# A planned three-stage kernel (attention, PReLU MLP, Mish MLP): a higher planned price on TensorE's mode changes, and a new table of priorities

## The chip, the cores and the metric

The kernel runs on one core of a Trainium2 chip. A core has four compute engines with instruction streams of their own: TensorE (PE; matmuls, its weight loads are listed as PEld), VectorE (DVE), ScalarE (ACT) and GpSimd (POOL). SyncE (SP) issues the DMAs here. Engines wait for each other through semaphores. SBUF is the memory on the core, PSUM the eight banks that the matmuls write. The metric is the device time of one execution in microseconds (us); lower is better. About 0.2% (some 2.1 us) is what repeated measurement can tell from no change.

## The reference

Three computations follow each other, all in float32 (the weights arrive as 64-bit floats):

```python
# attention: B=4, H=8, S=576, D=64
scores = (q @ k.T) / sqrt(D)
cum    = cumsum(log(clip(f, 1e-4, 1)), axis=-1)
scores = where(causal, -1e9, scores + cum[..., :, None] - cum[..., None, :])
attn   = exp(scores - max(scores)); attn /= sum(attn) + 1e-9
x = (attn @ v) -> 2304 tokens x 512
# MLP 1: 512 -> 2048 -> 512
h = x @ w_in;  g = max(h, 0) + alpha * min(h, 0);  x = g @ w_out
# MLP 2: 512 -> 2048 -> 512
h = x @ w_in;  g = h * tanh(log1p(exp(min(h, 20))));  out = g @ w_out
```

## The kernel before

**Attention** works on 16 pairs of heads. `stage_M` (L616) makes the scores once only for the row maximum, which VectorE takes from the bank (L623); its banks are 4 to 6, "one" in the planner. L635 transposes the maxima. `stage_S` (L660) makes the scores again, with bias and maximum folded in, in banks 0 to 3; ScalarE's Exp (L670) reads them, GpSimd selects (L678) and adds (L696). `stage_R` (L708) makes the row sums, ScalarE inverts them (L713, L716), VectorE scales (L718, L721). `stage_V` (L742) multiplies by v in banks 4 to 6, and VectorE writes the result to X (L748).

TensorE runs in three tilings, which the planner calls modes: r (whole array: L616, L635 and all of the MLPs), k (halves of 64 rows: L660) and c (halves of 64 columns: L708, L742).

**The MLPs** run over blocks of 384 tokens (6 blocks) and chunks of 128 of the 2048 hidden features (16 chunks). Every float32 product is made of three matmuls, high by high, high by low and low by high parts: a chunk's first product takes 12 matmuls (L786, L787, L788 for each of 4 slices of 128), its second 12 in layer 1 (L851 to L853) and 9 wider ones in layer 2 (L862 to L864). Splitting into parts is a cast on ScalarE (L321) and a subtraction (L331, `minus`) on GpSimd or VectorE. A PReLU is a Relu on ScalarE (L805) or a minimum on VectorE (L807), then L811 or L814 on VectorE, then that split: cast (L321) and subtraction (L331) make the two parts of g, which the second product reads.

The first four chunks of layer 1 are "group A". For blocks 0 to 2 they run as filler between the matmuls of attention, through bank 7 alone; for blocks 3 to 5 they run after attention's end (about 276 to 340 us). Then come the other 12 chunks of layer 1, six blocks of them (72 PReLUs; stage `H0`; to about 600 us); L905 folds a block's four output banks into what group A left. Then layer 2 (stage `H1`).

**Weights** arrive as 64-bit floats and are made into 32-bit ones half a tile at a time by ScalarE (L399) and VectorE (L401, L403, L405) in two buffers, wb. During layer 1 the weights of layer 2 are converted too and stored to DRAM (L434, `wd<-wb`); L399 of the next tile in the same buffer waits until that store has landed.

**What sets the order.** No engine chooses anything at run time. Every operation is first noted by `Plan.add` (L66) with its engine, a cost and a due time; the due time is shifted by `PRIO[stage][n]` for the n-th operation of a stage (L20), and where an operation can go to several engines, `ENG` (L21) picks one. `Plan.schedule` (L96) then builds one fixed sequence by list scheduling, and all engines' programs are written in it. Two numbers speak of TensorE's modes: `STAY` (L39) is added to the due time of an operation whose mode is not the present one, and `SWITCH` (L38) is added to the planned end of an operation that changes it.

```python
choice = [(p[0][0] + (self.STAY if m[0] != now[e] else 0.0), m) for m, p in open_[e].items()
...
end = free[e] = s + cost[n] + (self.SWITCH if m[0] != now[e] else 0.0)
```

Of the kernel before, what the change touches and what calls it, by code (L numbers as in the profile page):

```python
# [1041 lines left out]
```

## Time and profile before

| | us |
|---|---|
| median of 3 runs (range) | 1057.97 (1057.28 to 1059.17) |
| the profiled execution's own time | 1058.0 |
| its span in the profile | 1056.2 |
| TensorE busy | 1017.5 (96%) |
| VectorE busy | 745.1 (71%) |
| ScalarE busy | 542.1 (51%) |
| GpSimd busy | 414.2 (39%) |

The span runs from the first to the last record; 1.8 us of the execution lie outside it. "Busy" counts instructions under way, so short gaps between matmuls of different kinds show as idle time. Of the waits that the views list, only those of TensorE lengthen the span directly.

### The profile page before, as it was taken

Reading aid. Unit: us, or ns where it says so; the run is one execution under the profiler, and the core shown is the slowest. Engines: PE = TensorE matmul, PEld = TensorE weight load, DVE = VectorE, ACT = ScalarE, POOL = GpSimd, SP = SyncE. Lnnn points to the kernel's source line nnn. Section 1 sums busy time; section 2 is a strip of 40 time slices with the busy share of each in tenths; the row PEclk is TensorE's granted clock in tenths of the full one; section 3 lists DMA queues with packets and bytes.
Section 4 is the critical chain, followed back from the end, with each engine's and each line's share of the span. In section 5 each row is a group of like instructions: output and inputs, shape, how many; then the busy total and the mean of one; then the engine's idle time right before and its main releaser. Section 6 shows DMA issues by size and latency. Waiting matters only on the chain.

```text
span 1056.2 us, 16992 instructions
## 1 busy us (share of the span) xinstructions
PE 1017.5 (96%) x5996; PEld 914.7 (87%) x5996; DVE 745.1 (71%) x1673; ACT 542.1 (51%) x1133; POOL 414.2 (39%) x423
## 2 busy tenths in 40 slices
PE   7989999999978999999999999999999999999998
PEld 7756677777778999999999999998999989999897
DVE  6587655656588767888612247979888788887885
ACT  4777656664454544444332336555455454554543
POOL 4575543553455562413232324242233322423231
PEclk9999999999999999999999999999999999999999
DMA  5233221210133345565500034100000000000000
GB/s 163 89 110 98 79 70 36 71 48 12 44 117 100 125 137 183 183 207 182 163 1 1 20 92 129 41 1 31 1 6 25 1 30 1 1 31 1 31 1 31
DMA packets 55399, 71.06 MB, mean 67 GB/s; under 512 B 6673, under 2 KB 32273, under 8 KB 55313
## 3 DMA queue, kind: packets, MB, share of 16 engines
q1 hardware_dynamic: 55312, 69.97, 21.2%
q8 instruction: 47, 0.77, 0.3%
q14 instruction: 40, 0.32, 0.1%
HBM read 56.60 MB, written 13.33 MB: 66 GB/s over the span
## 4 chain that ended last, share of the span: by engine, by line
PE 85%; DVE 6%; DMA 3%; ACT 2%; issue 2%; POOL 1%; SPq 0%; ACTq 0%; DVEq 0%; POOLq 0%
PE b L786 12%; PE b L787 11%; PE b L788 11%; PE b L660 6%; PE b L863 6%; PE b L862 6%; PE b L864 6%; PE b L851 5%; PE b L853 5%; PE b L852 5%; PE b L742 4%; PE b L616 3%; PE b L519 2%; DVE wb L403 2%; PE b L708 2%
## 5 line engine op out<-in xcount | busy, mean ns | idle before, releaser
L786 PE MATMUL b<-xh,w 128*128 128x384 f32 x768 | 261.1, 340 | 9.0 <-ACT x L321 5.4
L788 PE MATMUL b<-xl,w 128*128 128x384 f32 x768 | 258.7, 337 | 0.0
L787 PE MATMUL b<-xh,w 128*128 128x384 f32 x768 | 258.6, 337 | 0.0
L843 POOL TENSOR_TENSOR x<-x 128x384 f32<-128x384 f32 x96 | 112.5, 1172 | 246.6 <-DVE x L841 165.7
L786 PEld LDWEIGHTS b<-xh,w 128*128 128x128 f32 x768 | 145.2, 189 | 17.6 <-ACT x L321 6.4
L787 PEld LDWEIGHTS b<-xh,w 128*128 128x128 f32 x768 | 145.2, 189 | 4.0
L788 PEld LDWEIGHTS b<-xl,w 128*128 128x128 f32 x768 | 145.0, 189 | 0.0
L331 POOL TENSOR_TENSOR g<-X,g 128x384 fp32r<-128x384 f32 x72 | 78.6, 1095 | 164.8 <-ACT g L321 128.4
L851 PE MATMUL b<-g,w 128*128 128x384 f32 x384 | 131.8, 343 | 9.4 <-DVE x L811 2.5
L853 PE MATMUL b<-g,w 128*128 128x384 f32 x384 | 129.8, 338 | 0.7 <-POOL g L331 0.6
L852 PE MATMUL b<-g,w 128*128 128x384 f32 x384 | 129.3, 337 | 0.0
L321 ACT CAST g<-x 128x384 fp32r<-128x384 f32 x120 | 61.4, 512 | 115.5 <-POOL x L843 105.0
L864 PE MATMUL b<-w,g 128*128 128x512 f32 x288 | 113.2, 393 | 0.0
L863 PE MATMUL b<-w,g 128*128 128x512 f32 x288 | 113.2, 393 | 0.0
L862 PE MATMUL b<-w,g 128*128 128x512 f32 x288 | 113.1, 393 | 0.0
L811 DVE SCALAR_TENSOR_TENSOR X<-X,alph,b 128x384 f32<-128x384 f32 x72 | 43.9, 611 | 84.3 <-ACT X L805 83.8
L623 DVE CUSTOM_DVE_ANT_0 junk<-b,tri 128x320 f32<-128x320 f32 (+3 forms) x160 | 69.4, 434 | 45.8 <-PE b L616 33.2
L331 DVE TENSOR_TENSOR g<-x,g 128x384 fp32r<-128x384 f32 x102 | 74.9, 736 | 17.6 <-ACT g L321 17.3
L399 ACT ACTIVATE wb<-raw 128x256 f32<-128x256 f32 x128 | 52.2, 432 | 66.8 <-DMA wd<-wb 38.2
L851 PEld LDWEIGHTS b<-g,w 128*128 128x128 f32 x384 | 72.6, 189 | 13.8 <-DVE x L814 3.4
L805 ACT ACTIVATE X<-b 128x384 f32<-128x384 f32 x72 | 35.2, 489 | 88.7 <-PE b L788 88.0
L401 DVE TENSOR_SCALAR wb<-wb 128x256 int32<-128x256 int32 x128 | 55.1, 450 | 33.9 <-ACT wb L399 33.0
(93 smaller groups left out, 1973.7 us busy)
## 6 DMA issues: line engine op xcount, KB each, us to landing
raw<-in_moe_w_in_dram SPq DMA_DIRECT2D x64, 256.0 KB
raw<-in_moe_w_out_dram SPq DMA_DIRECT2D x64, 256.0 KB
wd<-wb SPq DMA_DIRECT2D x32, 256.0 KB
raw<-wd SPq DMA_DIRECT2D x32, 256.0 KB
qt<-in_q_dram SPq DMA_DIRECT2D x16, 288.0 KB
kt<-in_k_dram SPq DMA_DIRECT2D x16, 288.0 KB
out_dram<-x SPq DMA_DIRECT2D x18, 256.0 KB
vt<-in_v_dram SPq DMA_DIRECT2D x16, 256.0 KB
```

The costliest lines, as they stand in the source:

```text
L331: plan.add(engs, 0.0, at, lambda e: (nc.gpsimd if e == "POOL" else nc.vector).tensor_tensor(out=out(), in0=in0(), in1=in1(), op=ALU.subtra ...
L623: nc.vector.tensor_tensor_reduce(out=junk[ql, :z - a], in0=ps()[ql, :z - a], in1=tri[ql, x0 + a:x0 + z], scale=-1.0, scalar=BIG if n == 0 ...
L786: nc.tensor.matmul(ps[:, :NB], w[:, 0, c], xh[c], start=(c == 0), stop=False)
L787: nc.tensor.matmul(ps[:, :NB], w[:, 1, c], xh[c], start=False, stop=False)
L788: nc.tensor.matmul(ps[:, :NB], w[:, 0, c], xl[c], start=False, stop=(c == KC - 1))
L843: add("POOL", c_pool(NB, 2.2), lambda e, m: nc.gpsimd.tensor_tensor(out=m, in0=e, in1=m, op=ALU.mult), [ek, mk], [mk])
L851: nc.tensor.matmul(ps[:, :NB], w[:, 0, c], g[:, 0], start=first, stop=False)
L852: nc.tensor.matmul(ps[:, :NB], w[:, 1, c], g[:, 0], start=False, stop=False)
L853: nc.tensor.matmul(ps[:, :NB], w[:, 0, c], g[:, 1], start=False, stop=last)
L862: nc.tensor.matmul(ps, g[:, 0, sl], w[:, 0], start=first, stop=False)
L863: nc.tensor.matmul(ps, g[:, 0, sl], w[:, 1], start=False, stop=False)
L864: nc.tensor.matmul(ps, g[:, 1, sl], w[:, 0], start=False, stop=last)
```

## The change

All of the diff is in the planner's numbers; no line that computes is touched. `SWITCH` rises from 0.2 to 0.3 us and `STAY` from 1.5 to 2.5 us. The table of shifts goes from 160 entries in 25 stages to 230 in 39, and most of the old entries have new values; the table of engines from 18 entries to 39. The entries of stage H0 (0 to 3 are the four slices of a chunk's first product, 4 the Relu, 5 L811, 6 the cast of g, 7 the subtraction) stand here for all:

```diff
-PRIO = {'': {0: -9.5, 1: -5.5, 2: -6, 3: -6.5, 4: -3.5},
...
- 'H0': {0: -11, 1: -10.5, 2: -12.5, 3: -43, 4: -1, 5: 6.5, 6: 1.5},
...
-ENG = {('A0g', 0): 'ACT', ('A1g', 0): 'ACT', ('A2g', 3): 'DVE',
...
+PRIO = {'': {0: -17.5, 1: -17.2, 2: -11, 3: -11.5, 4: -11.4},
...
+ 'H0': {0: -1, 1: -0.5, 2: -2.5, 3: -33, 4: 9, 5: 16.5, 6: 11.5, 7: 10},
...
+ENG = {('A0g', 0): 'ACT', ('A0g', 2): 'ACT', ('A0g', 3): 'POOL',
...
+ ('H0', 4): 'ACT', ('H0', 7): 'DVE', ('H1', 13): 'ACT', ('H1', 14): 'DVE',
...
-    SWITCH = 0.2
-    STAY = 1.5
+    SWITCH = 0.3
+    STAY = 2.5
```

What the planner makes of them: TensorE executes the same matmuls in another order, with 117 changes of mode instead of 134. 72 subtractions (L331, the low part of g in stage H0, one for each PReLU) move from GpSimd to VectorE, and six copies from a bank move from ScalarE to VectorE. Three places show the moves. In all rows b_65 to b_72 are banks 0 to 7.

First TensorE, in attention, near the 400th row of its order. Before, the row sums (L708) and two of the products with v (L742), both in mode c, stand apart, with filler (L851 to L853) and a row-maximum matmul (L616) in mode r and four score matmuls (L660) in mode k between them:

```order
L708 MATMUL b_67<-Pt_122,ones 64x128 x2
L708 MATMUL b_67<-accp,ones 64x160 x2
L708 MATMUL b_68<-accp,ones 64x288 x2
L851 MATMUL b_72<-g_105,w_1_83 128x384
L852 MATMUL b_72<-g_105,w_1_83 128x384
L853 MATMUL b_72<-g_105,w_1_83 128x384
L616 MATMUL b_71<-KM_1_135,QM_1_131 128x256
L660 MATMUL b_65<-qt_125,kt_128 128x288
L660 MATMUL b_66<-qt_125,kt_128 128x288
L660 MATMUL b_65<-BQ_141,BK_139 128x288
L660 MATMUL b_66<-BQ_141,BK_139 128x288
L742 MATMUL b_70<-Pt_122,vt_145 64x256 x2
```

In the changed kernel such pieces stand together (same stretch of the order): all of a pair's L742 and L708 in one run of mode c, and 16 score matmuls in a row just before it (not shown), and scores again behind it:

```order
L742 MATMUL b_70<-Pt_122,vt_145 64x320 x6
L742 MATMUL b_70<-Pt_122,vt_145 64x192 x2
L742 MATMUL b_70<-Pt_122,vt_145 64x64 x2
L708 MATMUL b_65<-Pt_122,ones 64x128 x2
L708 MATMUL b_65<-accp,ones 64x160 x2
L708 MATMUL b_66<-accp,ones 64x288 x2
L742 MATMUL b_69<-Pt_122,vt_145 64x256 x2
L742 MATMUL b_69<-Pt_122,vt_145 64x128 x2
L660 MATMUL b_67<-qt_125,kt_128 128x320
L660 MATMUL b_68<-qt_125,kt_128 128x320
```

Between the first L708 and the last L742 there were three changes of mode, and now there is none. Runs of L616 grow with it: of more than three in a row (the transposes L635 between them not counted) there were 9 and are 11, and the matmuls beyond the third in such runs were 19 and are 26. The L616 share three banks, so the fourth of a run waits for VectorE's reading of the first.

Second VectorE, where attention ends. The copy of bank 7 (L323) empties it after filler of group A; L718, L721 and L748 are the last pair's scaling; L401 to L405 a conversion of weights:

```order
L323 COPY x_2_117<-b_72 128x384
L718 SCALAR_TENSOR_TENSOR b_65<-b_65,rr 128x288
L718 SCALAR_TENSOR_TENSOR b_66<-b_66,rr 128x288
L721 SCALAR_TENSOR_TENSOR uu<-b_65,rr 128x288
L721 SCALAR_TENSOR_TENSOR uu<-b_66,rr 128x288
L748 SCALAR_TENSOR_TENSOR X<-b_70,uu 128x320
L748 SCALAR_TENSOR_TENSOR X<-b_69,uu 128x256
L807 TENSOR_SCALAR x_3_2639<-b_72,alph 128x384
L814 SCALAR_TENSOR_TENSOR x_3_2639<-b_72,x_3_2639 128x384
L401 TENSOR_SCALAR wb_92<-wb_92 128x256 x2
L403 SCALAR_TENSOR_TENSOR wb_92<-raw_91,wb_92 128x256 x2
L405 SCALAR_TENSOR_TENSOR wb_92<-raw_91,wb_92 128x256 x2
```

In the changed kernel the copy stands between the two L721, because the last 12 matmuls of filler now run after L708 and the last four L742, not ahead of them:

```order
L721 SCALAR_TENSOR_TENSOR uu<-b_67,rr 128x288
L323 COPY x_2_117<-b_72 128x384
L721 SCALAR_TENSOR_TENSOR uu<-b_68,rr 128x288
L748 SCALAR_TENSOR_TENSOR X<-b_71,uu 128x320
L748 SCALAR_TENSOR_TENSOR X<-b_70,uu 128x256
L807 TENSOR_SCALAR x_3_2636<-b_72,alph 128x384
L814 SCALAR_TENSOR_TENSOR x_3_2636<-b_72,x_3_2636 128x384
L401 TENSOR_SCALAR wb_92<-wb_92 128x256 x2
L403 SCALAR_TENSOR_TENSOR wb_92<-raw_91,wb_92 128x256 x2
L405 SCALAR_TENSOR_TENSOR wb_92<-raw_91,wb_92 128x256 x2
L401 TENSOR_SCALAR wb_2640<-wb_2640 128x256 x2
L403 SCALAR_TENSOR_TENSOR wb_2640<-raw_2639,wb_2640 128x256 x2
```

The first matmul after attention (L786, into bank 7) now stands behind this copy, where it did not before; and a second conversion (wb_2640) stands where the first kernel has the two L811 of its next rows.

Third ScalarE, in layer 1. The brackets name the engines and DMA queues that a row waits for (what follows the underscore only tells semaphores apart). Before, a Relu (L805) is followed by casts (L321) of PReLUs of two to three chunks earlier, which wait for TensorE to release the buffer g:

```order
L805 ACTIVATE X<-b_69 128x384 [waits PE_49,Pool_49]
L399 ACTIVATE wb_92<-raw_91 128x256 [waits DMAHW1_49,DMAHW0_49,DVE_49]
L321 CAST g_106<-X 128x384 [waits PE_49]
L399 ACTIVATE wb_92<-raw_91 128x256 [waits DMAHW2_49,DVE_49]
L399 ACTIVATE wb_2643<-raw_2642 128x256 [waits DMAHW4_49,DMAHW3_49,DVE_49]
L805 ACTIVATE X<-b_70 128x384 [waits PE_49,Pool_49]
L321 CAST g_107<-X 128x384 [waits PE_49]
L399 ACTIVATE wb_2643<-raw_2642 128x256 [waits DMAHW5_49,DVE_49]
L399 ACTIVATE wb_92<-raw_91 128x256 [waits DMAHW7_49,DMAHW6_49,DVE_49]
L399 ACTIVATE wb_92<-raw_91 128x256 [waits DMAHW0_49,DVE_49]
L805 ACTIVATE X<-b_71 128x384 [waits PE_49,Pool_49]
L321 CAST g_104<-X 128x384 [waits PE_49]
```

In the changed kernel the cast that follows is of the same PReLU and waits for VectorE's L811:

```order
L805 ACTIVATE X<-b_70 128x384 [waits PE_49,Activation_49]
L399 ACTIVATE wb_2640<-raw_2639 128x256 [waits DMAHW2_49,DVE_49]
L321 CAST g_105<-X 128x384 [waits DVE_49]
L399 ACTIVATE wb_92<-raw_91 128x256 [waits DMAHW4_49,DMAHW3_49]
L399 ACTIVATE wb_92<-raw_91 128x256 [waits DMAHW5_49]
L805 ACTIVATE X<-b_71 128x384 [waits PE_49,Activation_49]
L321 CAST g_106<-X 128x384 [waits DVE_49]
L399 ACTIVATE wb_2640<-raw_2639 128x256 [waits DMAHW7_49,DMAHW6_49]
L399 ACTIVATE wb_2640<-raw_2639 128x256 [waits DMAHW0_49]
L805 ACTIVATE X<-b_72 128x384 [waits PE_49,Activation_49]
L399 ACTIVATE wb_92<-raw_91 128x256 [waits DMAHW2_49,DMAHW1_49]
L321 CAST g_107<-X 128x384 [waits DVE_49]
```

The second product of a chunk now follows its first by 21 to 24 matmuls nearly everywhere in layer 1; before by 51 to 72, and by 30 to 33 at three boundaries between blocks. The L399 that wait for a landed store stand between the Relus in both kernels.

## Rows read from the trace of the kernel before

**Rows 1.** Page, part 1: busy us of each engine, share of the span, instructions.

```profile
PE 1017.5 (96%) x5996; PEld 914.7 (87%) x5996; DVE 745.1 (71%) x1673; ACT 542.1 (51%) x1133; POOL 414.2 (39%) x423
```

**Rows 2.** Windows: stretch, length, busy of PE, PEld, DVE, ACT, POOL, clock, DMA, GB/s.

```profile
25.00:280.00 255.00, 243.12 (x1833) 182.63 (x1832) 155.28 (x542) 158.57 (x328) 130.64 (x161) 1.00 0.22 66
...
300.00:304.00 4.00, 3.42 (x11) 3.42 (x12) 3.35 (x7) 1.05 (x3) 1.50 (x1) 0.57 0.46 150
410.00:515.00 105.00, 102.56 (x589) 101.73 (x589) 87.91 (x190) 46.65 (x110) 31.96 (x31) 1.00 0.60 193
600.00:1040.00 440.00, 440.00 (x2263) 404.88 (x2263) 357.17 (x627) 231.67 (x466) 145.82 (x125) 1.00 0.08 26
```

**Rows 3.** Waits of TensorE, 25 to 280 us (us in total, times, longest).

```profile
PE b L616 <- DVE M L623: 2.7, 6, 0.7
PE b L616 <- DVE nmx L623: 1.8, 4, 1.1
PE b L786 <- DVE x L811: 1.7, 3, 0.8
```

**Rows 4.** Waits of TensorE, 280 to 346 us.

```profile
PE b L786 <- ACT x L321: 5.4, 2, 4.1
PE b L851 <- DVE x L811: 2.5, 1, 2.5
...
PE b L786 <- DVE X L748: 1.4, 1, 1.4
```

**Rows 5.** Waits of TensorE, 346 to 600 us.

```profile
PE b L851 <- ACT g L321: 2.2, 1, 2.2
PE b L851 <- DVE x L905: 1.3, 1, 1.3
PE b L851 <- ACT wb L399: 1.1, 1, 1.1
```

**Rows 6.** Timeline of TensorE at 265.7 us (start, length, engine, line, instruction).

```profile
265.70 0.33 PE L852 MATMUL b<-g,w 128*128 128x384 f32 x1
265.87 0.34 PE L853 MATMUL b<-g,w 128*128 128x384 f32 x1
266.14 0.76 PE L660 MATMUL b<-qt,kt 64*128 64x288 f32 x4
```

**Rows 7.** Timeline, end of attention, 274 to 281 us.

```profile
274.29 0.56 DVE L323 COPY x<-b 128x384 f32<-128x384 f32 x1 [2.59 <-PE b L853]
...
276.21 0.39 PE L708 MATMUL b<-Pt,ones 128*64 128x128 f32 x4
...
277.29 0.45 PE L786 MATMUL b<-xh,w 128*128 128x384 f32 x1
...
278.66 0.83 DVE L718 SCALAR_TENSOR_TENSOR b<-b,rr 128x288 f32<-128x288 f32 x2 [3.82 <-ACT rr L716]
...
279.40 0.81 DVE L721 SCALAR_TENSOR_TENSOR uu<-b,rr 128x288 f32<-128x288 f32 x2
...
281.12 0.44 PE L786 MATMUL b<-xh,w 128*128 128x384 f32 x1 [1.45 <-DVE X L748]
```

**Rows 8.** Timeline of ScalarE before the longest wait of TensorE.

```profile
299.42 0.75 ACT L399 ACTIVATE wb<-raw 128x256 f32<-128x256 f32 x2 [2.99 <-POOL w L331]
```

**Rows 9.** Waits of ScalarE, 300 to 530 us.

```profile
ACT wb L399 <- DMA wd<-wb: 38.2, 21, 4.4
```

**Rows 10.** Timeline of one PReLU of layer 1 (ScalarE).

```profile
398.78 0.48 ACT L805 ACTIVATE X<-b 128x384 f32<-128x384 f32 x1
...
399.94 0.51 ACT L321 CAST g<-X 128x384 fp32r<-128x384 f32 x1
```

**Rows 11.** Groups of VectorE by line, 410 to 515 us (busy us, mean ns).

```profile
L403 DVE SCALAR_TENSOR_TENSOR wb<-raw,wb 128x256 int32<-128x256 int32 x52 | 28.9, 577 | 0.3
```

**Rows 12.** Timeline of VectorE at 338 us, with no GpSimd beside it.

```profile
337.94 0.54 DVE L331 TENSOR_TENSOR g<-x,g 128x384 fp32r<-128x384 f32 x1
338.40 0.41 DVE L403 SCALAR_TENSOR_TENSOR wb<-raw,wb 128x256 int32<-128x256 int32 x1
```

More of the change, by code (lines that the diff above doesn't have):

```diff
@@ L21 @@
-ENG = {('A0g', 0): 'ACT', ('A1g', 0): 'ACT', ('A2g', 3): 'DVE', ('AX', 1): 'DVE', ('AX', 3): 'DVE', ('AX', 5): 'DVE', ('AX', 7): 'DVE', ('B3', 4): 'DVE', ('H0', 4): 'ACT', ('H1', 14): 'DVE', ('O1', 5): 'DVE', ('WF', 2): 'DVE', ('X0', 1): 'POOL', ('X0', 3): 'POOL', ('X0', 7): 'POOL', ('X1', 3): 'POOL', ('X1', 5): 'POOL', ('X1', 7): 'POOL'}
+PRIO = {'': {0: -17.5, 1: -17.2, 2: -11, 3: -11.5, 4: -11.4}, 'A0': {0: -1.0, 1: -1, 2: 7.5, 3: -8.5}, 'A0g': {1: -13.5, 2: -16.5, 3: -21.1}, 'A1': {0: 50, 1: -24.7, 2: 1, 3: -42.4}, 'A1g': {0: -16.6, 1: 5, 2: 6, 3: -0.2}, 'A2': {0: 48.5, 2: -4, 3: 15.2}, 'A2g': {0: 12, 1: -22.0, 2: 30.6, 3: 15}, 'A3': {0: 9.5, 1: -8, 2: -42.3, 3: -28.5}, 'A3g': {0: 31, 1: 4, 2: 54.2, 3: -6}, 'AX': {1: 10.1, 2: 21.5, 3: -5, 4: 12, 5: 11.5, 6: 25.1, 7: 21}, 'B0': {0: 1.3, 1: -1.3, 2: 2, 3: 8, 4: -1}, 'B1': {0: 0.5, 2: -26.9, 3: 2, 4: -17.3}, 'B2': {0: 4.5, 1: 0.5, 2: -31.4, 3: 7.5, 4: 8.5}, 'B3': {0: -15.7, 1: 24, 2: -57.2, 3: 7, 4: 1.5, 5: -3.5, 6: 1.4, 7: 2.5}, 'H0': {0: -1, 1: -0.5, 2: -2.5, 3: -33, 4: 9, 5: 16.5, 6: 11.5, 7: 10}, 'H1': {0: -45.2, 1: -4.5, 2: -40.5, 3: -36.5, 4: -2.5, 5: 4.5, 6: 1, 7: 8, 8: -70.4, 9: -7.1, 10: 3.7, 11: -4, 12: -33.6, 13: -5.5, 14: -30.5}, 'LB2': {0: -1.6, 1: 2, 2: 2, 3: 2}, 'LQ2': {0: -38.9, 1: 20}, 'LV2': {0: 6.3, 1: 20}, 'M2': {0: 20, 1: 6.1, 2: 20, 3: 27.7, 4: 20, 5: 20, 6: 20, 7: -2.4, 8: 20, 9: 21.2, 10: 16.0, 11: 47.1, 12: 20, 13: 30.5, 14: 20, 15: 20, 16: 20, 17: 20, 18: 20, 19: 30.1, 20: 20, 21: 20.5, 22: 20, 23: 20.6}, 'NM2': {0: 0.6, 2: 4.6}, 'O0': {0: -1, 1: -8.5, 2: -11.1, 3: -37, 4: 29.1, 5: 2.5, 6: -0.5, 7: -0.1}, 'O1': {0: -8.5, 1: 22.5, 2: 17.4, 3: 41.2, 4: -9.7, 5: 25, 6: 15.8, 7: 36.5, 8: 62.5}, 'R2': {6: -0.3, 7: -4.9, 9: -1.8, 10: 3.8, 11: -25.5}, 'ST0': {1: 3.2, 3: -4.8}, 'ST1': {0: -6.4, 2: -1.6}, 'ST2': {2: -17.2}, 'ST3': {3: 53.3}, 'T2': {0: -5, 1: -5, 2: -5, 3: -5}, 'W': {0: 36.6, 1: -4, 2: -12.5, 3: -7.6, 4: 34, 5: -33.3, 6: -58.3, 7: 9.5, 8: 30, 9: -6.5, 10: -29.8, 11: -5, 12: 1, 13: -25.9}, 'WA': {0: 2, 1: 4.0, 3: -24.8, 4: -10.5, 5: 6.5, 6: 2, 7: 5, 8: -41.5, 9: -12.9, 10: -6.3, 11: 10.8, 12: 7.5}, 'WF': {0: 33.9, 1: 5.4, 2: -47.5}, 'WS': {0: 1, 1: 4.2, 2: -17, 3: -56, 4: -2, 5: -12.8, 6: -1.4, 7: -6.7, 8: -15.5, 9: -26, 10: -6.8, 11: -40.8, 13: -5.5}, 'X0': {0: -1.6, 1: -52.2, 2: 38.0, 3: -5, 4: -2, 5: 11.5, 6: 22.0, 7: -19.1}, 'X1': {0: -10.8, 1: -14.4, 2: -13.2, 3: -22, 4: -4.5, 5: 16.4, 6: -22.5, 7: -49.3}, 'alph': {0: 60.6, 1: 32.4}, 'const': {0: 46.5, 1: 2}, 'pro2': {1: -42.3, 3: -16.0, 7: -1.2, 8: -7.9, 11: 10.3, 12: 7.7, 13: 19.7, 18: -5.1, 21: -1.9, 22: 17.9, 24: -4.5, 25: 15.7, 26: -9.5, 27: 35.1}, 'warm2': {0: 6.0}}
@@ new lines @@
+ENG = {('A0g', 0): 'ACT', ('A0g', 2): 'ACT', ('A0g', 3): 'POOL', ('A1g', 0): 'ACT', ('A2g', 2): 'ACT', ('A2g', 3): 'DVE', ('A3g', 0): 'DVE', ('AX', 1): 'DVE', ('AX', 2): 'ACT', ('AX', 3): 'DVE', ('AX', 4): 'ACT', ('AX', 5): 'DVE', ('AX', 7): 'DVE', ('B0', 4): 'DVE', ('B3', 4): 'DVE', ('H0', 4): 'ACT', ('H0', 7): 'DVE', ('H1', 13): 'ACT', ('H1', 14): 'DVE', ('NM2', 1): 'ACT', ('NM2', 2): 'ACT', ('O1', 3): 'DVE', ('O1', 5): 'ACT', ('R2', 3): 'POOL', ('T2', 2): 'ACT', ('T2', 3): 'ACT', ('WF', 2): 'DVE', ('X0', 0): 'ACT', ('X0', 1): 'POOL', ('X0', 2): 'ACT', ('X0', 3): 'POOL', ('X0', 4): 'ACT', ('X0', 6): 'ACT', ('X0', 7): 'POOL', ('X1', 0): 'ACT', ('X1', 3): 'POOL', ('X1', 5): 'POOL', ('X1', 6): 'ACT', ('X1', 7): 'POOL'}
```

1 line of the change is left out of this document (removed).

## The prediction

> **What bounds the kernel now.** I read the page first: TensorE is busy for 1017.5 us, 96% of the span of 1056.2; no other engine is over 71% [rows 1]. So a saving must come out of the 38.7 us in which TensorE is idle, or out of time in which it is busy but slow. Then the windows, to find where those are [rows 2]. In attention it is busy for 243.12 of 255 us. Late in layer 1 and in layer 2 (600 to 1040 us) it is busy all of the time at a granted clock of 1.00, with no wait: nothing can be won there, only lost. Then its waits, stage by stage: small ones in attention, on VectorE's reading of row maxima (2.7 and 1.8 us) and on PReLU results for the filler (1.7) [rows 3]; 5.4, 2.5 and 1.4 us where attention ends and group A goes on [rows 4]; 2.2, 1.3 and 1.1 us at the first three boundaries between blocks of layer 1 [rows 5]. Last the clock: right after the wait of 4.1 us, from 300 to 304 us, the granted clock averages 0.57, so most of that stretch ran at the lower of the two levels (1.2 GHz), and 3.42 us of matmuls there did 0.57 times 3.42 of full-speed work: 1.5 us lost [rows 2]. Two more windows look the same, after the waits of 2.5 and 2.2 us; the waits of up to 1.4 us are followed by none. So a wait of over 2 us costs its length and about 1.5 us more.
>
> The profiled execution took 1058.0 us, the median of the runs is 1057.97: I sum against 1058.0 and correct nothing.
>
> **The change part by part.** The work is the same, so each term is a wait that goes, comes or changes size. The order shows which rows stand ahead of which; lengths are from rows.
>
> *Mode changes.* Two matmuls of 384 columns start 0.17 us apart, and over the change from r to k it is 0.27: 0.10 us for a change [rows 6]. 17 fewer: -1.7 us. Bounds: 0, if a wait for banks takes the place of each, and -4.6 (17 times 0.27, as if the whole step went).
>
> A rule bears on this: the Trainium skill, "TensorEngine Tiling (Array Packing)", Key Properties, says that a change of tiling mode drains TensorE. A full drain would let the next matmul start when the last, 0.34 us long, has ended, 0.17 us later than usual; by that the term would be -2.9. The row shows the next one starting 0.07 us before that end, so the measured 0.10 stands.
>
> *Bank 7.* The filler's first products wait 1.7 us for L811 [rows 3]. In the new order the distances from a chunk's end to the next use of bank 7 fall short less often (by my count the shortfalls sum to about half). I take -1.0; bounds 0 and -1.7.
>
> *Longer runs of L616.* The two waits on L623 make 4.5 us [rows 3]. Matmuls beyond the third in a run go from 19 to 26; in proportion the waits become 6.2: +1.7. Bounds 0 and +4.5.
>
> *End of attention.* L786 waited 1.4 us, until L748 had freed a bank [rows 4]. Now 12 matmuls of filler and four L742 stand between the last L708 and L786, so that wait goes; but L786 writes bank 7, whose copy on VectorE now stands behind the first L721. From the start of L708 (276.21) to the end of the first L721 it is 2.45 + 0.83 + 0.41 = 3.7 us; the L708 take 1.1 (to 277.29, where the next matmul starts), four L742 0.5 (as four L708 at 0.39, and a change of mode at each side), 12 matmuls at 0.17 2.1, so they end at 3.7 too, and the last one drains until 3.85; the copy takes 0.56 [rows 7]. L786 starts at 4.45 instead of 3.7: a wait of 0.75. Net -0.6; bounds -1.4 and +1.
>
> *The wait of 4.1 us at 300.6.* It ends on ScalarE's copy out of a bank. The copy stood behind L399, which had waited 2.99 us for GpSimd's w L331 [rows 8]. In the new order it still stands behind an L399 that waits for the same; but ahead of it GpSimd has other work done sooner. By my reading about 1.2 us go. Against that a second conversion now stands ahead of two L811, some 2 us of VectorE, at a place where TensorE has 1 to 1.5 us of cover: +0.5. Net -0.7; bounds -5.6 (wait and clock gone) and +3.
>
> *The wait of 2.5 us at 333.9.* It ended on an L811 behind a whole conversion [rows 4]; now both L811 of that block stand between halves of one. With its share of clock 4.0 us are there; the L807 and L814 behind them now follow a conversion instead, so I take -1.5. Bounds -4.0 and +1.
>
> *Boundaries in layer 1.* The 1.3 and 1.1 us end right after the fold L905 [rows 5]. From a block's last use of the fourth output bank to its first use for the next there were 12 matmuls each time; now 12, 39 and 45. The second and third go: -2.4; the first, with its 2.2 us and its clock, I leave. Bounds -6.1 and +2.
>
> *Shorter cover in layer 1.* 24 matmuls at 0.17 us are 4.1 us between the end of a chunk's first product and the first use of its g; before it was 51 to 72, 8.8 us and more [rows 6]. From the start of the Relu to the end of the cast it is 1.67 us [rows 10]; with the last matmul's drain (0.17) and, as an estimate from the gaps in these rows, 0.3 for signals that is 2.1, so 2.0 us of slack are left, or 1.2 where one pair of VectorE's conversions (0.8) is ahead. ScalarE's L399 waits 21 times for a landed store, 38.2 us in all, 1.8 in the mean [rows 9]. Queued behind such an L399 are the Relu or the cast of the present chunk; with the old cover no one missed them. If every wait came as before, each would exceed the slack by 0.6: 21 times 0.6, +12.6 us. But from the store's issue to the L399 that needs it there are now about two chunks, 8.3 us. I take +2, near the lower end; bounds 0 and +12.6.
>
> *72 subtractions from GpSimd to VectorE.* Alone one takes 0.54 us there [rows 12]. From 410 to 515 us VectorE is busy for 87.91 of 105 us [rows 2]; 25 of these (one for each chunk of 24 matmuls, 4.1 us) add 13.5, which would make 101.4. On the other side L403 takes 577 ns in the mean there, against 0.41 us with no GpSimd beside it [rows 11, 12]; 52 of them at 0.41 give back 8.7 us. VectorE ends at some 93 us of 105: off the path, cost 0; the price if that cover is gone is part of the second rival.
>
> The Trainium skill, "SBUF — State Buffer", Who interferes with whom, says that VectorE and GpSimd contend for a shared pair of ports under an exclusive lock, and for nothing else. The 577 against 410 ns agree. By that rule more comes back, on L401 and L405 too; without it VectorE would be at 101.4 of 105 and the second rival the likeliest.
>
> *Layer 2.* No wait before, and the distances in the new order are longer: 0.
>
> Sum: -1.7 - 1.0 + 1.7 - 0.6 - 0.7 - 1.5 - 2.4 + 2.0 = -4.2, so **1053.8 us**.
>
> **The rivals.**
>
> *Nothing to measure.* Attention is bound by TensorE's matmuls and its bank waits, so mode changes are replaced by waits: runs of L616 cost twice my term (+3.4), bank 7 gains nothing, and the transition keeps its waits under other names. 1058.0 - 1.7 + 3.4 - 0.6 - 2.4 + 2.0 gives 1058.7. For it: the waits at 300.6 and 333.9 depend on engines whose queues hardly changed there. Against it: many old waits would have to be matched.
>
> *Slower: the short cover.* Place: ScalarE in layer 1, at L399 behind the stores. It decides from the point where an L399 waits more than 1.2 us for its landing, and the mean was 1.8 [rows 9]. Without my +2 the sum is -6.2; +12.6 makes 1064.4. For it: one of these waits was 4.4 us. Against: stores are now issued two chunks ahead of the L399 that needs them, so such waits should be rarer and shorter.
>
> *Much faster.* The transition's waits in rows 4 all go (9.3 us) with two of the clock's falls (3.0), the rest as forecast: 1058.0 - 1.7 - 1.0 + 1.7 - 9.3 - 3.0 - 2.4 + 2.0 = 1044.3. For it: they are single waits, each one misplaced row. Against: the queue ahead of the copy at 300.6 is nearly the same.
>
> **How the numbers follow.** Forecast 0.50 (own range 1049 to 1059), nothing to measure 0.20, slower 0.17, much faster 0.13. The range of 8 in 10 reaches into both outer cases: 1045.5 to 1063. A difference of under 0.2% (2.1 us: 1055.9 to 1060.1) can't be told from none. Faster: 0.42 of the forecast's 0.50, 0.03 of the second case, all 0.13: 0.58. Same: 0.07, 0.12 and 0.02: 0.21. Slower: 0.01, 0.05 and 0.15: 0.21.
>
> **What would show it.** TensorE's waits on L623 in attention near 6 us; a wait of about 0.75 on the copy of bank 7 where attention ends, none on L748; at the next two places a wait of 2.5 to 3.5 us, and one of 1 us or less, with one window of low clock fewer; the second and third boundary without a wait; L403's mean nearer to 0.41 us. In layer 1 the sign of the short cover is L851 waiting for g L321: none or a few within 2 us in all by the forecast, a dozen or more by the slower rival. The forecast is wrong if new waits come up after 600 us, or if attention's end moves later.

## The result, and the profile after

| | before | changed |
|---|---|---|
| median, us (runs) | 1057.62 (4) | 1042.97 (4) |
| range, us | 1056.53 to 1059.17 | 1042.02 to 1045.02 |
| profiled execution: own time; span, us | 1058.0; 1056.2 | 1045.0; 1043.3 |
| attention's last matmul ends at, us | 277.4 | 276.0 (12 filler matmuls, 2.1 us, are left) |
| last L853 of group A starts at, us | 346.5 | 335.9 |
| last L853 of layer 1 starts at, us | 662.0 | 650.2 |

The ratio is 0.986 (95% interval 0.984 to 0.988): 14.6 us faster, where 4.2 were forecast; 1043.0 lies below the range. It is 1.3 us from the number of the rival "much faster" (1044.3). Where the time went, by the two profiled executions (12.9 us apart; the changed one is the slowest of its four): attention gave nothing (its end is 1.4 us earlier, with 2.1 us of work left over), the stretch from there to group A's end (69.1 us before, 59.9 now) gave 9 us, and behind it 2.3 us came, 1.1 of them after layer 1's last L853.

Windows of the changed kernel that answer to [rows 2] (columns as there):

```profile
25.00:280.00 255.00, 242.02 (x1827) 183.31 (x1826) 154.81 (x547) 156.77 (x327) 131.80 (x161) 0.99 0.22 67
300.00:304.00 4.00, 4.00 (x25) 4.00 (x24) 2.56 (x8) 2.22 (x6) 3.28 (x2) 1.00 0.71 241
410.00:515.00 105.00, 104.96 (x605) 104.47 (x604) 85.43 (x221) 48.67 (x112) 6.72 (x6) 1.00 0.67 210
```

From 300 to 304 us the granted clock stays at 1.00 where it was 0.57. In attention it fell instead. These are two windows of the kernel before, then the same two of the changed kernel:

```profile
70.00:75.00 5.00, 5.00 (x42) 3.34 (x38) 2.79 (x14) 4.74 (x12) 2.96 (x5) 1.00 0.35 108
100.00:105.00 5.00, 5.00 (x48) 3.34 (x46) 3.42 (x10) 4.16 (x10) 2.18 (x4) 1.00 0.14 42
```

```profile
70.00:75.00 5.00, 5.00 (x31) 3.77 (x30) 3.13 (x15) 3.50 (x10) 1.32 (x2) 0.71 0.35 111
100.00:105.00 5.00, 5.00 (x29) 3.38 (x31) 3.60 (x16) 2.63 (x8) 0.45 (x2) 0.66 0.01 2
```

TensorE is busy all of the time in both, so 0.29 and 0.34 of 5 us are lost: about 3 us, an estimate from these rows. All four profiled executions with this attention show both falls (att_new, after_sub_pool and mode_price below too); of the ten with the old attention eight show one, near 96 us, and this one none.

From 410 to 515 us VectorE is busy for less time than before (85.43 against 87.91 us) although 25 subtractions came to it, and TensorE has no gaps left there.

TensorE's waits in attention (as [rows 3]):

```profile
PE b L616 <- DVE M L623: 4.9, 10, 1.0
PE b L616 <- DVE X L748: 2.7, 2, 1.9
PE b L660 <- ACT Pt L670: 1.7, 4, 0.5
PE b L616 <- DVE nmx L623: 1.5, 6, 0.4
PE b L786 <- DVE x L811: 0.5, 1, 0.5
```

The two waits on L623 make 6.4 us (forecast 6.2), the one for bank 7 (L786 on L811) fell from 1.7 to 0.5. Two more grew that the prediction did not have: L616 on L748 (1.1 before) and L660 on the Exp L670 (not in the list before). All listed waits of the window make 12.3 us, 10.3 before.

The waits from 280 to 346 us (as [rows 4]), and the only one behind them (as [rows 5]):

```profile
PE b L786 <- ACT x L321: 2.1, 1, 2.1
PE b L851 <- DVE x L814: 1.4, 1, 1.4
PE b L851 <- ACT g L321: 1.2, 1, 1.2
PE b L853 <- POOL g L331: 0.5, 1, 0.5
PE b L853 <- DVE g L331: 0.4, 1, 0.4
```

```profile
PE b L851 <- DVE x L905: 1.9, 1, 1.9
```

Behind group A the first boundary alone is left; no L851 waits for a cast of g there, though the cover is 24 matmuls. The end of attention came out as forecast (as [rows 7]): L786 waits for the copy of bank 7, which stands between the two L721.

```profile
277.83 0.45 DVE L721 SCALAR_TENSOR_TENSOR uu<-b,rr 128x288 f32<-128x288 f32 x1
278.42 0.56 DVE L323 COPY x<-b 128x384 f32<-128x384 f32 x1
...
279.04 0.45 PE L786 MATMUL b<-xh,w 128*128 128x384 f32 x1 [0.72 <-DVE x L323]
```

0.72 us, where 0.75 was worked out. And two rows of layer 1: L403's mean (as [rows 11]), and ScalarE's waits for landed stores (as [rows 9]), 38.2 us before.

```profile
L403 DVE SCALAR_TENSOR_TENSOR wb<-raw,wb 128x256 int32<-128x256 int32 x53 | 21.6, 420 | 0.5
```

```profile
ACT wb L399 <- DMA wd<-wb: 16.1, 13, 4.2
```

### The profile page after: what moved, and what is told of

The parts are those of the page before. It is cut to its first block, busy times and chain, and to the rows that moved or that the text cites. A ratio compares the mean times of both kernels' runs of the same rounds, so it can differ in the third digit from the quotient of the medians.

```text
span 1043.3 us, 16906 instructions
## 1 busy us (share of the span) xinstructions
PE 1013.2 (97%) x5996; PEld 914.6 (88%) x5996; DVE 745.3 (71%) x1751; ACT 541.1 (52%) x1127; POOL 338.2 (32%) x351
## 4 chain that ended last, share of the span: by engine, by line
PE 85%; DVE 7%; ACT 2%; DMA 2%; issue 2%; POOL 1%; DVEq 0%; SPq 0%; ACTq 0%; POOLq 0%
PE b L786 12%; PE b L788 12%; PE b L787 12%; PE b L864 6%; PE b L863 6%; PE b L862 6%; PE b L851 6%; PE b L853 5%; PE b L852 5%; PE b L660 5%; PE b L742 3%; PE b L616 3%; PE b L519 2%; DVE junk L623 2%; PE b L708 2%
## 5 line engine op out<-in xcount | busy, mean ns | idle before, releaser
L786 PE MATMUL b<-xh,w 128*128 128x384 f32 x768 | 259.3, 338 | 3.3 <-ACT x L321 2.1
L786 PEld LDWEIGHTS b<-xh,w 128*128 128x128 f32 x768 | 144.5, 188 | 8.7 <-ACT x L321 2.4
L851 PE MATMUL b<-g,w 128*128 128x384 f32 x384 | 130.3, 339 | 4.8 <-DVE x L905 1.9
L853 PE MATMUL b<-g,w 128*128 128x384 f32 x384 | 129.2, 336 | 0.9 <-POOL g L331 0.5
L321 ACT CAST g<-x 128x384 fp32r<-128x384 f32 x120 | 61.4, 513 | 106.1 <-POOL x L843 54.9
L623 DVE CUSTOM_DVE_ANT_0 junk<-b,tri 128x320 f32<-128x320 f32 (+3 forms) x160 | 69.3, 433 | 44.1 <-PE b L616 31.8
L331 DVE TENSOR_TENSOR g<-x,g 128x384 fp32r<-128x384 f32 x102 | 73.7, 726 | 37.7 <-ACT g L321 37.1
L811 DVE SCALAR_TENSOR_TENSOR X<-X,alph,b 128x384 f32<-128x384 f32 x72 | 43.9, 612 | 70.6 <-ACT X L805 70.0
L805 ACT ACTIVATE X<-b 128x384 f32<-128x384 f32 x72 | 35.1, 490 | 90.4 <-PE b L788 90.0
L331 POOL TENSOR_TENSOR xl<-X,xh 128x384 fp32r<-128x384 f32 x18 | 20.3, 1137 | 188.9 <-ACT xh L321 188.7
L851 PEld LDWEIGHTS b<-g,w 128*128 128x128 f32 x384 | 72.2, 188 | 6.9 <-ACT X L805 2.2
L853 PEld LDWEIGHTS b<-g,w 128*128 128x128 f32 x384 | 72.4, 188 | 1.9 <-DVE g L331 1.1
L670 ACT ACTIVATE Pt<-b 128x512 f32<-128x512 f32 (+1 forms) x128 | 56.2, 503 | 32.6 <-PE b L660 29.2
```

What stands on the lines that cost most here:

```text
L331: plan.add(engs, 0.0, at, lambda e: (nc.gpsimd if e == "POOL" else nc.vector).tensor_tensor(out=out(), in0=in0(), in1=in1(), op=ALU.subtra ...
L623: nc.vector.tensor_tensor_reduce(out=junk[ql, :z - a], in0=ps()[ql, :z - a], in1=tri[ql, x0 + a:x0 + z], scale=-1.0, scalar=BIG if n == 0 ...
L786: nc.tensor.matmul(ps[:, :NB], w[:, 0, c], xh[c], start=(c == 0), stop=False)
L851: nc.tensor.matmul(ps[:, :NB], w[:, 0, c], g[:, 0], start=first, stop=False)
L853: nc.tensor.matmul(ps[:, :NB], w[:, 0, c], g[:, 1], start=False, stop=last)
```

## Experiments: which stage

Every experiment uses the kernel's own planner; what differs is said with each. Intervals are 95%; each ratio is to the kernel before on the same chip.

| run | median, us | ratio to before |
|---|---|---|
| att_new | 1057.4 | 1.000 (0.999 to 1.001) |
| rest_new | 1044.1 | 0.987 (0.985 to 0.989) |
| l1_new | 1053.2 | 0.996 (0.994 to 0.997) |
| one_sub | 1056.6 | 0.999 (0.998 to 1.001) |
| one_move | 1057.9 | 1.000 (0.998 to 1.001) |
| prelu_first | 1058.4 | 1.001 (1.000 to 1.002) |
| before_sub_dve | 1054.3 | 0.996 (0.994 to 0.998) |
| after_sub_pool | 1047.2 | 0.990 (0.988 to 0.991) |
| mend3 | 1051.3 | 0.993 (0.992 to 0.995) |
| w_later | 1048.6 | 0.992 (0.990 to 0.994) |
| w_sooner | 1044.9 | 0.988 (0.986 to 0.990) |
| knobs_only | 1045.3 | 0.989 (0.987 to 0.991) |
| tables_only | 1031.0 | 0.976 (0.973 to 0.978) |
| att_cheap | 1036.4 | 0.981 (0.979 to 0.982) |

Three kernels join the two orders: one up to a point, and from there what is left in the sequence of the other.

```diff
-        for n in order:
-            ops[n][3]()
...
+        cut = max(one.index(n) for n in self.marks["swap1"])
+        head = one[:cut + 1]
+        done = set(head)
...
+        for n in head:
+            self.alt[0][n][3]()
+        for n in two:
+            if n not in done:
+                self.alt[1][n][3]()
```

In att_new `one` is the order of the changed kernel and `two` that of the kernel before; in rest_new it is the other way round; both are cut at attention's end. l1_new is as rest_new, cut at group A's last matmul (`self.marks["ga"]`).

> The changed kernel's order up to the end of attention, and from there what is left in the order of the kernel before (its engines too). Theory T (read from the two traces): the gain lies behind attention, where TensorE loses 9.7 us less until 346 us and 2.9 less in layer 1, while attention itself is 0.7 us longer; so this kernel takes about 1058, between 1056 and 1060. Rival R: the stages hang together, the state in which attention leaves the queues (12 matmuls of filler left over as cover, the weights' loads) makes the quick transition; then it takes 1052 or less.

> The other half: the order of the kernel before up to the end of attention, and from there what is left in the changed kernel's order. Theory T: nearly the whole gain, 1042 to 1045. Rival R (the state that attention leaves makes the transition): 1048 or more, since the cover of 12 left matmuls is missing and the conversions stand elsewhere.

> The order of the kernel before up to its last matmul of group A (about 346 us), then what is left in the changed order: layer 1's short cover, the 72 subtractions on VectorE, layer 2. Theory T, from the traces: layer 1 gives 2.9 us and layer 2 1.1, so 1053 to 1055, and the difference to the other half is the transition. Rival: the short cover and the subtractions pay for themselves only with the changed transition in front; then 1057 or more.

All three came out by theory T: the new attention is worth nothing (-0.2 us), the new rest nearly all (-13.5), layer 1 and 2 alone -4.4. So about 9 us (13.5 less 4.4) belong to the stretch between attention's end and group A's end (the transition), and the stages hardly depend on each other.

## Experiments: single waits of the transition

The prediction had priced that stretch wait by wait. Three edits of the kernel before take away the cause of one wait each. The first moves one operation, the subtraction that GpSimd runs at 295.86 us, to VectorE:

```diff
+OVER = {1712: 'DVE'}
...
+                e = engs.get(key, next(iter(eng)))
+                e2 = OVER.get(n, OVER.get(key, e))
+                pick.append((e, eng[e], at + prio.get(key[0], {}).get(key[1], 0.0), lambda f=fn, e=e2: f(e)))
```

> The kernel before with one instruction on another engine, its place in the order kept: the subtraction w L331 that GpSimd runs at 295.86 for 3.53 us goes to VectorE. Theory T2: the wait of 4.1 us at 300.6 hangs on that one stretched instruction; without it ScalarE's L399 and the copy behind it come 1.1 to 2 us sooner, the wait is 2 to 3 us, and with the clock staying up 1 to 3.5 us are gained: 1054.5 to 1057. Rival: the L399 would wait for its raw weights anyway (their DMAs are issued at 295.4), or VectorE's 0.9 us more delays the conversion just as long: no change, 1057 to 1059.

Its timeline (ScalarE, TensorE):

```profile
298.98 0.43 ACT L399 ACTIVATE wb<-raw 128x256 f32<-128x256 f32 x1 [1.24 <-DMA raw<-in_moe_w_in_dram]
...
300.44 0.45 PE L786 MATMUL b<-xh,w 128*128 128x384 f32 x1 [2.60 <-ACT x L321]
```

The wait shrank from 4.07 to 2.60 us, and then L399 waited for its DMA instead of GpSimd. The profiled run had won 2.4 us until group A's end and lost as much again at the first boundary of layer 1. The time, 1056.6, lies in the range of T2, but its interval takes in no change: it is not told apart from before.

The second edit moves one L811 ahead of the conversion that it stood behind:

```diff
+        for n, m in [(1614, 1800)]:
+            rest.remove(n)
+            rest.insert(rest.index(m), n)
```

> The kernel before with one VectorE instruction moved: the L811 that runs at 333.20 goes ahead of the two L403 and two L405 that stand before it (behind the two L401). Theory T4: the wait of 2.5 us at 333.9 goes and the clock stays up there: 2 to 4 us, 1053.5 to 1056. Rival (seen with the moved subtraction, where 2.4 us were won until 346 us and 2.1 lost again at 400 us): the boundary at 400 us is set by the weights' conversion and not by TensorE, and takes back what was won: 1056.5 to 1058.5, with the wait at 402 us grown.

```profile
331.11 0.60 DVE L811 SCALAR_TENSOR_TENSOR x<-x,alph,b 128x384 f32<-128x384 f32 x1
...
334.19 0.62 ACT L321 CAST w<-wb 128x512 fp32r<-128x512 f32 x1 [2.58 <-DVE wb L405]
334.72 0.51 ACT L321 CAST g<-x 128x384 fp32r<-128x384 f32 x1
...
335.33 0.44 PE L851 MATMUL b<-g,w 128*128 128x384 f32 x1 [2.54 <-DVE x L814]
```

The time, 1057.9, lies in the rival's range, but the reason is another: L811 ran 2.1 us sooner (331.11 against 333.20, in a run whose attention ended 1.4 us later), and TensorE waited just as long (2.54 against 2.45 us). On ScalarE the cast of g stood behind the cast of w, which waits for the same conversion's last L405. The same profile shows what such a wait is worth: the wait of 4.07 us at 300.6, which this edit does not touch, was 2.63 us there. TensorE had come to it later, after a stretch at a lower clock, and the matmul that ends it started 23.2 us after attention's end in both runs. What TensorE had lost before cost nothing up to there.

The third edit mends both queues:

```diff
+        for n, m in [(1614, 1800), (1621, 1800), (1622, 1800), (1615, 1807), (1623, 1807)]:
```

> The kernel before with five instructions moved. One L811 moved alone won nothing: the wait of 2.5 us at 334 stayed, now on the cast of g behind ScalarE's cast of w, which waits for the same conversion, and on an L814 behind it. Here that L811, the L807 and L814 after it go ahead of the conversion's two L403 and two L405 on VectorE, and both casts of g ahead of the cast of w on ScalarE. Theory T4: the conversion in front of the PReLUs, on both engines, makes that wait; it falls from 2.5 to 1 us or less, with the clock up there: 1054 to 1056.5. Rival: the conversion comes 1.8 us later, and this is paid back in full at the boundary at 400 us: 1057 to 1060.

```profile
337.22 0.55 DVE L331 TENSOR_TENSOR g<-x,g 128x384 fp32r<-128x384 f32 x1
...
337.82 0.52 PE L853 MATMUL b<-g,w 128*128 128x384 f32 x1 [3.60 <-DVE g L331]
```

That wait went, and 4 us later a longer one (3.6 us) came on a subtraction behind the conversions that had been put off. T4 fell: in the kernel before, to take one row away does not take the time away. A wait that moves on when its cause is taken away suggests that an engine as a whole is late, here VectorE, on whose results these waits end, directly or through ScalarE's casts. The next runs test that.

## Experiments: VectorE's conversions

If VectorE is late, what counts may be how much conversion work stands in the transition. VectorE's share there is not the 71% of the whole span; it was busy for 56.32 of 66 us, 85%, in the kernel before:

```profile
280.00:346.00 66.00, 54.46 (x282) 51.14 (x283) 56.32 (x119) 33.92 (x80) 32.06 (x26) 0.95 0.34 106
```

In the table half tiles are the L405 of the stretch; the time is the sum over L401, L403 and L405; idle is the stretch less TensorE's busy time. Each row is one profiled execution. rest_new is the control of w_sooner, the kernel before the control of w_later.

| kernel, stretch (us) | length | TensorE idle | half tiles | L401+L403+L405, us | clock |
|---|---|---|---|---|---|
| before, 277.0 to 346.5 | 69.5 | 11.9 | 28 | 41.0 | 0.95 |
| knobs_only, 277.4 to 339.9 | 62.5 | 7.5 | 24 | 34.8 | 0.95 |
| rest_new, 277.4 to 337.8 | 60.4 | 7.3 | 22 | 29.8 | 0.97 |
| w_sooner, 278.1 to 343.8 | 65.7 | 6.7 | 27 | 34.3 | 0.95 |
| w_later, 278.7 to 338.9 | 60.2 | 4.2 | 24 | 30.3 | 0.97 |
| changed, 275.7 to 335.9 | 60.2 | 6.3 | 22 | 28.9 | 1.00 |
| tables_only, 267.7 to 324.5 | 56.8 | 3.7 | 18 | 28.4 | 1.00 |

Two kernels shift the due times of stage W, the load and conversion of layer 1's weights, in what is planned behind attention:

- w_later: the tables of the kernel before, every entry of `PRIO['W']` 10 us later;
- w_sooner: the changed tables and numbers, every entry of `PRIO['W']` 20 us sooner.

> The kernel before up to attention's end; behind it the same tables and numbers, but the due times of all operations of stage W (load and conversion of layer 1's weights) 10 us later. 22 half conversions then stand ahead of the end of group A instead of 28, the number of the changed kernel. Theory V: between attention's end and group A's end VectorE is the bound, and that stretch is as long as the conversions in it make it: 28 took 69.6 us (71.0 with the other attention), 24 62.6, 22 60.2 and 60.5, 18 56.8; so it becomes 60 to 62 us and the kernel 1048 to 1052. Rival: the tables' finer order makes the transition, and the count only goes along with it, or conversions that come later are missed in layer 1's first block: 1055 or more.

> The kernel before up to attention's end, then the changed tables and numbers (with those tables unshifted this took 1044), but stage W due 20 us sooner: 26 half conversions ahead of group A's end, not 22. Theory V: the stretch is 65 to 68 us instead of 60.5, the kernel 1048 to 1052. Rival (order, not count): 1042 to 1046.

w_later came out by theory V (with 24 half tiles, where 22 were expected): one number for a whole stage, no row chosen by hand, gives 8.5 us. But it does not change the conversions alone, since the planner orders all that stands behind attention anew, and behind group A TensorE's waits grew from 4.6 to 6.2 us.

w_sooner speaks against V: the stretch became 65.7 us as expected, but the time stayed at 1044.9, in the range of the rival (order, not count) and not told apart from rest_new's 1044.1. In that stretch TensorE also did more (316 matmuls against 291 in rest_new), so the length says little; its idle time, 6.7 us, is not above rest_new's 7.3, with five half tiles and 4.5 us of conversion more. The groups of VectorE in the transition, first before, then w_sooner:

```profile
L405 DVE SCALAR_TENSOR_TENSOR wb<-raw,wb 128x256 int32<-128x256 int32 x28 | 14.6, 560 | 0.0
L403 DVE SCALAR_TENSOR_TENSOR wb<-raw,wb 128x256 int32<-128x256 int32 x28 | 14.1, 540 | 0.0
L401 DVE TENSOR_SCALAR wb<-wb 128x256 int32<-128x256 int32 x28 | 12.3, 471 | 6.2 <-ACT wb L399 6.1
```

```profile
L403 DVE SCALAR_TENSOR_TENSOR wb<-raw,wb 128x256 int32<-128x256 int32 x28 | 12.0, 467 | 0.0
L401 DVE TENSOR_SCALAR wb<-wb 128x256 int32<-128x256 int32 x28 | 12.0, 463 | 3.8 <-ACT wb L399 3.8
L405 DVE SCALAR_TENSOR_TENSOR wb<-raw,wb 128x256 int32<-128x256 int32 x27 | 10.3, 415 | 0.0
```

The 28 instructions of L405 and of L403 cost 560 and 540 ns in the mean there, and 415 and 467 here. Taken one by one, every L405 with no GpSimd instruction beside it took 414 to 422 ns in both kernels; in the kernel before eight had one beside them and took 924 ns in the mean.

So neither the number nor the time of the conversions alone is the measure. Over the whole table TensorE's idle time falls with the conversions' time (11.9 us with 41.0, 3.7 with 28.4), but not from row to row (7.3 with 29.8, 6.7 with 34.3, 4.2 with 30.3). Shown is that the order behind attention's end makes the 9 us, and that taking away the priced causes one by one does not. That VectorE's conversions are what paces the stretch rests on w_later and on VectorE's share (81 to 87% in all seven rows) and is in part argued; a finer order of all engines is the rival that stands.

In layer 1 the same collision is taken away by the 72 subtractions, tested in both kernels by the line with `e2` above, every engine's order else kept (`OVER = {('H0', 7): 'DVE'}` in the kernel before, `'POOL'` in the changed one):

> The kernel before with one part of the change alone: the 72 subtractions of g's low part in layer 1 on VectorE and not GpSimd; every engine's order is else the same. Theory T3: GpSimd's subtractions stretch VectorE's conversions (L403 577 ns instead of 410), and these pace the chain load, L399, L401 to L405, store, on which the boundaries of layer 1 hang; with them gone the waits at 402, 455 and 507 us shrink by 1 to 4 us together: 1053.5 to 1056.5, and L403's mean falls to 430 or less. Rival: those waits hang on the fold L905 behind VectorE's queue, or on landings; 1056.5 to 1059.

> The changed kernel with the same 72 subtractions back on GpSimd, orders of TensorE and ScalarE unchanged. Theory T3: VectorE's conversions are stretched again (L403 over 520 ns); with only 24 matmuls of cover the Relu's chain is late a few times: 1045 to 1050. Rival: the cover of 4.1 us holds one GpSimd subtraction (1.1 us) as well, and VectorE has room: 1042 to 1044.5.

L403 in the window of [rows 11], with the subtractions on VectorE in the kernel before, then on GpSimd in the changed one:

```profile
L403 DVE SCALAR_TENSOR_TENSOR wb<-raw,wb 128x256 int32<-128x256 int32 x54 | 21.9, 427 | 0.3
```

```profile
L405 DVE SCALAR_TENSOR_TENSOR wb<-raw,wb 128x256 int32<-128x256 int32 x56 | 30.5, 558 | 0.5
L403 DVE SCALAR_TENSOR_TENSOR wb<-raw,wb 128x256 int32<-128x256 int32 x56 | 25.0, 460 | 0.6
```

Both times came out by T3: -4.2 us alone, and +3.4 when taken back (0.990 against 0.986). One sign of T3 did not: L403 was to be over 520 ns in after_sub_pool and was 460 (L405 558). With the subtractions moved alone, TensorE's waits from 346 to 600 us in the kernel before fell from 4.6 us [rows 5] to

```profile
PE b L853 <- DVE g L331: 1.5, 1, 1.5
```

at 386 us, and none of the three boundaries' waits is left, though the order is the old one. In the changed kernel with the subtractions back on GpSimd the waits of that stretch are these (1.9 us in the changed kernel):

```profile
PE b L851 <- ACT g L321: 2.3, 1, 2.3
PE b L852 <- POOL w L331: 0.8, 1, 0.8
PE b L853 <- POOL g L331: 0.5, 1, 0.5
PE b L788 <- POOL xl L331: 0.4, 1, 0.4
```

1.7 us of them end on GpSimd's own subtractions. So the 4 us are the subtractions' place, which is shown; how much of it comes by shorter conversions on VectorE and how much by a GpSimd that is free sooner, no run separates.

The three edits together:

> The kernel before with all three edits: the subtraction w L331 of 295.86 on VectorE, the L811 of 333.20 moved ahead, the 72 subtractions on VectorE. If the weights' conversion sets the boundary at 400 us and the 72 subtractions slow it (T3), then the three together give more than their sum: 1047 to 1052. Rival: each gain is taken back at 400 us, 1055 to 1058.

1051.3 is in the range of the expectation, 7.2 us faster (95% interval 5.0 to 8.9). The three alone make 5.8 (-1.0, -0.6 and -4.2), so that together they give more than their sum is not shown. Nor is it ruled out: against the subtractions alone the two edits of the transition bring 3 us here, where each alone brought 1.0 and 0.6 that could not be told from nothing.

## Experiments: the two numbers and the price of a mode change

knobs_only keeps the tables of the kernel before:

```diff
-    SWITCH = 0.2
-    STAY = 1.5
+    SWITCH = 0.3
+    STAY = 2.5
```

tables_only keeps the tables of the changed kernel and takes the same four lines the other way round.

> The tables of the kernel before with the two new numbers alone, SWITCH 0.3 and STAY 2.5: 125 changes of mode instead of 134. Theory T: attention's time does not follow the number of mode changes (17 fewer gave nothing), so 1056 to 1060 unless the transition or layer 1 happens to be ordered better. Rival: the dearer mode change is what makes the gain; then well under 1053.

> The changed tables with the old numbers, SWITCH 0.2 and STAY 1.5: 132 changes of mode; the 72 subtractions are on VectorE as in the changed kernel. Theory T: the gain lies in the tables' order behind attention, so most of it stays, 1043 to 1050. Rival: it comes from the two numbers; 1053 or more.

Theory T misses both times; the rival's number came out for knobs_only and not for tables_only. The two numbers alone win 12.2 us with the old tables, the tables alone 26.5 us with the old numbers, and both together 14.6: with the new tables the dearer mode change costs 11 to 12 us. tables_only beats both kernels of this case. L616's waits on L623 in its attention:

```profile
PE b L616 <- DVE M L623: 2.3, 6, 0.6
PE b L616 <- DVE nmx L623: 0.8, 3, 0.3
```

These are 3.1 us where the changed kernel has 6.4, with 132 changes of mode instead of 117. All listed waits of its attention make 4.1 us (12.3 in the changed kernel), and the granted clock is 1.00 all through it. The next run puts that attention in front of the changed rest. `one` is planned with the changed tables at `SWITCH` 0.2 and `STAY` 1.5, `two` as in the changed kernel, cut at attention's end.

> The changed kernel with attention alone planned at the old numbers (SWITCH 0.2, STAY 1.5, changed tables); behind it the changed order. With the old numbers everywhere the whole took 1031.0, and attention 8.9 us less than in the changed kernel, with 15 more changes of mode. Theory P: the dearer mode changes cost attention those 9 us in waits for banks; 1033 to 1036. Rival: that attention was quick only with what was planned behind it: 1040 or more.

1036.4, 0.4 beyond the range of theory P and far from the rival: the two numbers cost attention about 6 us of the time (0.981 against 0.986), and its end comes 8.1 us sooner (267.9 against 276.0). The other 5 us to tables_only lie behind attention.

The price itself, measured in one execution with nothing to wait for (`r_`, `k_` and `c_` issue one matmul, or pair, of each mode):

```diff
...
+    for p, q in ((r_, k_), (r_, c_), (k_, c_)):
+        for f in [p] * 24 + [q] * 24 + [p, q] * 24:
+            f()
```

> The changed kernel with 480 matmuls added behind its last instruction, whose results nobody reads: 24 in mode r (384 columns), 24 pairs in mode k (288 columns), then the same alternating; so too r with c (pairs of 64 columns in plain float32) and k with c. The difference between grouped and alternating, over 47 changes, is the price of a change without any wait. The prediction took 0.10 us; the spacings in attention give 0.20 in the mean. If the price is 0.20 in itself, 17 fewer changes are worth 3.4 us; if it is 0.10, the rest of the 0.20 is waiting that any order has.

The end of 24 in mode r, 24 pairs in mode k, and the two alternating:

```profile
1041.64 0.86 PE L1009 MATMUL b<-xh,w 128*128 128x384 f32 x4
1042.43 3.43 PE L1013 MATMUL b<-xh,w 64*128 64x288 f32 x48
1045.79 0.44 PE L1009 MATMUL b<-xh,w 128*128 128x384 f32 x1
1046.16 0.40 PE L1013 MATMUL b<-xh,w 64*128 64x288 f32 x2
1046.49 0.44 PE L1009 MATMUL b<-xh,w 128*128 128x384 f32 x1
```

In runs r takes 0.174 us and a k pair 0.136 (3.36 less one exit of 0.10, over 24). Alternating, the two take 0.70 (1045.79 to 1046.49): 0.39 for two changes, **0.195 each**. Half shows before the change, as in [rows 6] (0.79 for four r, 0.10 over); the other half in the first matmul after it, 0.44 long instead of 0.34. The granted clock was 1.00 there. With mode c on one side the same working gives 0.17.

## Why the prediction was wrong

*The transition: the steps at 300.6 and 333.9 failed.* They gave -0.7 and -1.5; the stretch gave 9. The prediction took each wait by itself, asked which row now stood ahead of its releaser, and priced that row. The runs show that taking such a row away moves the wait on: from 4.07 to 2.60 us with no time won that can be told (one_sub), from 2.45 to 2.54 (one_move), and to 3.60 us, 4 us later (prelu_first). What the prediction left out is VectorE's work in the stretch as a whole, 85% of it by the row above, since "no other engine is over 71%" was an average over the whole span. The conversions are the largest part of that work, 41.0 us before and 28.9 now; how far they are the cause stays open, as said above. With the waits, the clock's falls there went too (granted clock 0.95 before, 1.00 now). The rival "much faster" had the place, for the reason of single misplaced rows, which is not what was shown; that its number came so near is luck, for it had 12.3 us in the transition and nothing for the subtractions.

*The 72 subtractions: set at nothing, and worth 4.2 us.* The collision was seen, and L403 fell to 420 ns as worked out; but its worth was set at 0 because VectorE was held to be off the path. Measured alone it is -4.2 us. The reading of T3 is that VectorE's conversions pace the chain load, L399, conversion, store, on which the boundaries hang; it is argued, beside the GpSimd that is free sooner. The Trainium skill, "SBUF — State Buffer", Who interferes with whom, had it that the lock is exclusive; all three conversions got shorter (L401, L403 and L405, from 410 to 515 us: before 447, 577 and 479 ns; with the subtractions moved alone 300, 427 and 416).

*Short cover: +2 taken, nothing measured.* No L851 behind group A waits for a cast of g. ScalarE's waits for stores fell from 38.2 to 16.1 us; the longest is still 4.2, more than the slack of 1.2, and TensorE did not wait. So the slack as it was worked out does not decide; why, no run shows.

*Boundaries: the number right, the cause not alone.* The second and third are gone, the first stays (1.9 us, now on L905). The new distances are enough for that, since after_sub_pool has no wait at those two either; but so is the move of the subtractions, since before_sub_dve has none at all three with the old distances. The two do not add up: l1_new, with both, gives 4.4 us, the subtractions alone 4.2.

*Attention: the sum near by luck, the terms not.* A change costs 0.17 to 0.195, not 0.10, so 17 fewer are worth about 3 us. The listed waits took 2.0 of that back: L616 on L623 grew by 1.9 as forecast, L616 on L748 by 1.6 and L660 on L670 by 1.7, while bank 7 gave 1.2 (-1.0 was taken) and 2.1 us of L742's waits went. And the clock fell twice where it had not in the profile before, about 3 us (half of that against the executions of the old attention with one fall), which no term had. A rule that had been weighed, a full drain (the Trainium skill, "TensorEngine Tiling (Array Packing)", Key Properties), gave 2.9, by an estimate from rows: nearer than the 1.7 read from one spacing, which shows only the half before the change. That the new attention as a whole is worth nothing is shown by att_new (-0.2 us).

*End of attention: right*, 0.72 us, though the rows of the prediction add up to 4.41 and not 4.45. *Layer 2: nearly*, 1.1 us less, with no wait in either kernel.

What stays open: what of the order behind attention makes the transition's 9 us, and why the same two numbers help the one table and hurt the other. In attention they hurt by waits (12.3 against 4.1 us) and by the two falls of the clock, and 15 changes of mode fewer give back about 3 us; behind attention no run says.

## What to carry to other kernels

Where several waits stand close together on one engine's results, do not price them one by one: look at that engine's share in that stretch, not over the span, and try whether taking one cause away only moves the wait. An instruction moved away from an engine can be worth more than its own length, by what it gives back to the instructions beside it: VectorE got 25 subtractions more and was busy for less time. A planner's cost and its table of priorities are one setting: try each alone, since here each helped alone, and together they gave back almost half of what the table alone had won.
